# Moving the query and key transposes of a fused attention and MLP kernel from TensorE to the DMA engines

## The chip, the cores and the metric

The kernel runs on one core of one Trainium2 chip. The metric is the device time of one execution in microseconds (us). The executions of the kernel before lie within 0.5% of each other. Every ratio to the kernel before is of the same chip and the same rounds; where other runs are compared with each other or with the kernel after, they can be of different sessions, and the four sessions of the experiments were on four chips. The engines are named as the profile names them: PE is TensorE (PEld its weight loads), DVE is VectorE, ACT is ScalarE, POOL is GpSimd (its queue also issues DMAs that convert types) and SP is SyncE (its queue issues the other DMAs). L214 is line 214 of the kernel that the profile belongs to, so the same statement has other line numbers in other kernels.

## The reference

```python
def attention(q, k, v):                    # (8, 12, 448, 64), float32
    scores = (1 / sqrt(64)) * q @ k.T
    return (maximum(scores, 0) ** 2 / 448) @ v

x = attention(q, k, v)                     # heads side by side: (3584, 768)
out = maximum(x @ w_in, 0) ** 2 @ w_out    # w_in (768, 2048), w_out (2048, 768)
```

There is no softmax: attention is two matrix products with a squared ReLU between them, and the MLP has the same form.

## The kernel before

The work is ordered by batch (8) and pair of heads (6 a batch, so 48 pairs). For each pair, q and k come in as float32, are transposed on PE (so that the 64 head dimensions lie on partitions), and are copied by DVE into float16 tiles. Then come eight score matmuls (`sps`), a squared ReLU by ACT and DVE for each (`at`), and eight matmuls with v (`avps`). The MLP's matmuls (`hps` for the hidden layer, `ops` for the output) of earlier batches are a queue of filler that `fill` hands out between the attention's matmuls, so that PE has work while ACT and DVE are busy.

```python
    ps_p   = tile_pool(name="ps",   bufs=4, PSUM)   # sps, avps, hps: one bank each
    psmi_p = tile_pool(name="psmi", bufs=2, PSUM)   # tq, tk: one bank each
    pso_p  = tile_pool(name="pso",  bufs=1, PSUM)   # ops, 768 float32 columns: two banks
    FILL_RATIO = 1.5

    def attention_hp(b, hp):
        qst = qk_p.tile([SB, NSB, 2, D], FP32)      # SB = 112, NSB = 4
        kst = qk_p.tile([SB, NSB, 2, D], FP32)
        for j, vt in ((0, vA), (1, vB)):
            nc.sync.dma_start(out=qst[:, :, j, :], in_=q[b, 2*hp+j]...)
            nc.sync.dma_start(out=kst[:, :, j, :], in_=k[b, 2*hp+j]...)
            nc.gpsimd.dma_start(out=vt[...], in_=v[b, 2*hp+j, 0:384]...)
            nc.gpsimd.dma_start(out=vt[...], in_=v[b, 2*hp+j, 384:448])
        tq = psmi_p.tile([P, S], FP32)
        for i in range(NSB):
            nc.tensor.transpose(tq[:, i*SB:(i+1)*SB], qst[:, i], ident)
            fill(224)
        # two DVE copies into qTA and qTB (one head each, the other half zero), fill(500)
        # the same for kst: four transposes, one DVE copy into kT, fill(500)
        for c in range(4):
            for j, qT in ((0, qTA), (1, qTB)):
                sps = ps_p.tile([P, S], FP32)
                nc.tensor.matmul(sps, lhsT=kT[:, c*P:(c+1)*P], rhs=qT)
                # at <- sps by ACT and DVE
                fill(448)
        avps = ps_p.tile([P, S], FP32)
        # eight matmuls with v and at, fill(448) after each; ACT writes x
```

The PSUM has eight banks, and the three pools take all of them: 4 + 2 + 2. (The Trainium skill, "PSUM — Partial Sum Buffer", Specifications, gives 8 banks of 2 KiB a partition, so that the 768 float32 columns of `ops` need two.) A scheduler orders each engine's instructions when the kernel is built, by the readiness that it estimates, so the order in a queue is not the order of the source.

## Time and profile before

| | before |
|---|---|
| time, median of 6 runs at first (later sessions 538.07 to 539.49) | 538.97 us |
| PE busy | 500.0 of 538.4 us |
| start, batch 0's attention (cut at 63.7 us; its last `avps` ends at 65.0) | 63.7 us |
| middle, the 42 pairs of batches 1 to 7 (cut at 476.0 us; their last `avps` ends at 477.1) | 412.3 us |
| tail, MLP matmuls alone | 62.4 us |

The first lines are from the page of the kernel before: the span, PE's busy time with its share of the span and its count of instructions, and the engines' shares of the chain of work that ended last.

```profile
span 538.4 us, 8018 instructions
...
PE 500.0 (93%) x2816; PEld 281.6 (52%) x2816; DVE 373.4 (69%) x663; ACT 297.9 (55%) x589; POOL 138.4 (26%) x220
...
PE 87%; DMA 8%; ACT 2%; SPq 1%; DVE 1%; issue 0%; ACTq 0%
```

The windows view of the same kernel has the three stages. Its columns are the stretch in us, its length, each engine's busy time with its number of instructions, PE's granted clock (1.00 is full), the share of the DMA engines' time in use, and GB/s.

```profile
0.00:63.70 63.70, 38.20 (x148) 19.22 (x149) 37.95 (x72) 26.37 (x54) 30.66 (x56) 0.84 1.10 177
63.70:476.00 412.30, 409.43 (x2371) 233.37 (x2369) 324.89 (x576) 256.58 (x511) 107.77 (x164) 1.00 0.44 76
476.00:538.40 62.40, 52.38 (x300) 29.06 (x298) 10.60 (x18) 14.90 (x24) 0.00 (x0) 0.99 0.11 45
```

The profile counts PE as busy for 409 of the 412 us of the middle stage, so PE's work must shrink to save much time there. In the timeline of PE, each line is the start in us, the time taken, and what ran; x4 stands for four in a row.

```profile
206.62 0.35 PE L227 MATMUL sps<-qTA,kT 128*128 128x448 f16 x1
206.80 0.55 PE L217 MATMUL tk<-ident,kst 112*128 112x112 f32 x4
207.19 0.35 PE L227 MATMUL sps<-qTB,kT 128*128 128x448 f16 x1
```

The four transposes start at 206.80 and the next matmul at 207.19, so a transpose takes 0.097 us of PE, although the profile gives each one 0.27 us (its end is modelled and overlaps the next start). By the same reading a 448-column matmul takes 0.19 us, and 384 transposes take 37 us of the program's 473 us of PE work.

PE's waits after batch 0, from the table of waits with a window from 62 us to the end. The columns are the total in us, the number of waits and the longest.

```profile
PE ops L158 <- ACT osb L169: 7.4, 10, 0.9
PE sps L227 <- DVE at L114: 1.1, 6, 0.2
PE avps L236 <- DVE at L114: 0.2, 1, 0.2
```

Only one wait counts: `ops`, which has one PSUM buffer, waits for ACT to evict it. POOL waits for much longer (this line is for the whole program), but for nothing that holds anybody up: its v loads wait for the `avps` that used their tile.

```profile
POOL vf L197 <- PE avps L236: 273.2, 42, 9.4
```

### The profile page before, as it was taken

To read this page: it belongs to the slowest core of one execution; us is meant where nothing else is said; L and a number is where in the kernel's file an instruction comes from. 1 tells how busy PE (TensorE), PEld (TensorE's weight loads), DVE (VectorE), ACT (ScalarE), POOL (GpSimd) and SP (SyncE) were. 2 spreads that over 40 slices of the span, in tenths; PEclk is the share of its full clock that TensorE was granted. 3 is DMA by queue.
4 is the path that set the end of the run, shared out by engine and by line. 5 is a ranking of instruction groups with operands and counts; after the bars stand their busy time and mean duration, and the time that the engine had idled before them with its cause. 6 is when DMAs were issued, how large, how long until landed. Compare 5 with 4: busy or idle time off the path is not lost.

```text
span 538.4 us, 8018 instructions
## 1 busy us (share of the span) xinstructions
PE 500.0 (93%) x2816; PEld 281.6 (52%) x2816; DVE 373.4 (69%) x663; ACT 297.9 (55%) x589; POOL 138.4 (26%) x220
## 2 busy tenths in 40 slices
PE   1676999999999999999999999999999999999886
PEld 1333455555555555555555555555555555554553
DVE  2667788888887667898875667898875667764000
ACT  0444576667675546676745546675754555654111
POOL 7444311331133123213232123213232113000000
PEclk9968899999999999999999999999999999999999
DMA  9999534545355454343445454343545452100211
GB/s 162 199 205 197 79 50 72 82 86 93 62 85 89 95 119 67 46 78 47 82 89 104 93 118 66 48 69 51 78 96 94 106 109 36 10 0 3 86 60 59
DMA packets 142408, 45.36 MB, mean 84 GB/s; under 512 B 135968, under 2 KB 138016, under 8 KB 142368
## 3 DMA queue, kind: packets, MB, share of 16 engines
q1 hardware_dynamic: 93120, 33.04, 24.9%
q0 software_dynamic: 49248, 11.81, 22.6%
q8 instruction: 22, 0.36, 0.3%
q14 instruction: 18, 0.15, 0.1%
HBM read 45.61 MB, written 11.01 MB: 105 GB/s over the span
## 4 chain that ended last, share of the span: by engine, by line
PE 87%; DMA 8%; ACT 2%; SPq 1%; DVE 1%; issue 0%; ACTq 0%
PE hps L131 27%; PE ops L158 19%; PE sps L227 13%; PE avps L236 13%; PE ops L162 9%; DMA kst<-in_k_dram 6%; PE tq L208 3%; PE tk L217 3%; ACT osb L169 2%; DMA qst<-in_q_dram 2%; SPq L189 1%; ACT sq L113 1%; DVE at L114 1%; SPq L193 0%; ACTq L169 0%
## 5 line engine op out<-in xcount | busy, mean ns | idle before, releaser
L114 DVE SCALAR_TENSOR_TENSOR at<-sps,sq 128x448 f16<-128x448 f32 x384 | 216.1, 618 | 47.8 <-ACT sq L113 46.3
L113 ACT ACTIVATE sq<-sps 128x448 f16<-128x448 f32 x384 | 191.7, 550 | 78.3 <-PE sps L227 76.7
L131 PE MATMUL hps<-xt,w 128*128 128x448 f16 x768 | 188.0, 352 | 0.0
L158 PE MATMUL ops<-w,g 128*128 128x512 f16 x448 | 159.6, 379 | 7.6 <-ACT osb L169 7.4
L197 POOL DMA_DIRECT2D vf<-in_v_dram x96 | 74.2, 774 | 310.5 <-PE avps L236 273.2
L162 PE MATMUL ops<-w,g 128*128 128x256 f16 x448 | 122.0, 272 | 0.0
L236 PE MATMUL avps<-at,vf 128*128 128x448 f16 x384 | 111.3, 367 | 1.2 <-DVE at L114 1.0
L131 PEld LDWEIGHTS <-w 128*128 128x128 f16 x768 | 74.7, 97 | 69.7 <-issue 4.2
L113 ACT ACTIVATE sq<-hps 128x448 f16<-128x448 f32 x128 | 69.4, 542 | 58.2 <-PE hps L131 57.1
L114 DVE SCALAR_TENSOR_TENSOR g<-hps,sq 128x448 f16<-128x448 f32 x128 | 79.3, 620 | 32.0 <-ACT sq L113 31.7
L227 PE MATMUL sps<-qTA,kT 128*128 128x448 f16 x192 | 70.1, 365 | 1.6 <-DVE at L114 1.4
L227 PE MATMUL sps<-qTB,kT 128*128 128x448 f16 x192 | 69.9, 364 | 1.1 <-DVE at L114 1.1
L162 PEld LDWEIGHTS <-g 128*128 128x128 f16 x448 | 43.6, 97 | 34.5 <-issue 12.1
L158 PEld LDWEIGHTS <-g 128*128 128x128 f16 x448 | 43.5, 97 | 34.3 <-PE sps L227 0.4
L236 PEld LDWEIGHTS <-vf 128*128 128x128 f16 x384 | 38.6, 101 | 40.3 <-issue 8.6
L227 PEld LDWEIGHTS <-kT 128*128 128x128 f16 x384 | 36.8, 100 | 33.2 <-issue 6.2
L242 ACT ACTIVATE xt<-avps 128x448 f16<-128x448 f32 x48 | 26.0, 542 | 48.5 <-PE avps L236 48.0
L201 POOL DMA_DIRECT2D vf<-in_v_dram x96 | 52.3, 547 | 1.9 <-PE ops L158 0.9
L169 ACT ACTIVATE osb<-ops 128x768 f32<-128x768 f32 x28 | 22.8, 813 | 51.3 <-PE ops L162 51.3
L210 DVE TENSOR_SCALAR qTA<-tq 64x448 f16<-64x448 f32 x48 | 29.1, 606 | 29.7 <-PE tq L208 29.7
L208 PE MATMUL tq<-ident,qst 112*128 112x112 f32 x192 | 33.0, 269 | 14.0 <-DMA qst<-in_q_dram 13.2
L217 PE MATMUL tk<-ident,kst 112*128 112x112 f32 x192 | 35.5, 274 | 8.5 <-DMA kst<-in_k_dram 8.5
(17 smaller groups left out, 125.9 us busy)
## 6 DMA issues: line engine op xcount, KB each, us to landing
qst<-in_q_dram SPq DMA_DIRECT2D x96, 112.0 KB, 2.8
kst<-in_k_dram SPq DMA_DIRECT2D x96, 112.0 KB, 2.7
out_dram<-osb SPq DMA_DIRECT2D x28, 384.0 KB, 2.8
vf<-in_v_dram POOLq DMA_DIRECT2D x96, 48.0 KB, 2.6
w<-in_moe_w_in_dram POOLq DMA_DIRECT2D x6, 512.0 KB, 8.4
w<-in_moe_w_out_dram POOLq DMA_DIRECT2D x16, 192.0 KB, 8.3
vf<-in_v_dram POOLq DMA_DIRECT2D x96, 8.0 KB, 2.4
```

What stands on the lines that cost most here:

```text
L113: nc.scalar.activation(out=sq[:n], in_=src[:n], func=AF.Square)
L114: nc.vector.scalar_tensor_tensor(out=dst[:n], in0=src[:n], scalar=0.0, in1=sq[:n], op0=ALU.is_gt, op1=ALU.mult,)
L131: nc.tensor.matmul(hps[0], lhsT=w1[m][:, f * P : (f + 1) * P], rhs=xt[m][:, b * S : (b + 1) * S], start=(m == 0), stop=(m == NDMT - 1),)
L158: nc.tensor.matmul(ops[0][:, 0:512], lhsT=gt[f][:, rs], rhs=w2[f][:, 0:512], start=(f == 0), stop=(f == NFFT - 1),)
L162: nc.tensor.matmul(ops[0][:, 512:768], lhsT=gt[f][:, rs], rhs=w2[f][:, 512:768], start=(f == 0), stop=(f == NFFT - 1),)
L169: nc.scalar.activation(out=osb, in_=ops[0], func=AF.Copy, scale=CO)
L197: nc.gpsimd.dma_start(out=vt[:, 0:3, j * 64 : j * 64 + 64], in_=v[b, 2 * hp + j, 0:384].rearrange("(c p) d -> p c d", p=P),)
L201: nc.gpsimd.dma_start(out=vt[0:64, 3, j * 64 : j * 64 + 64], in_=v[b, 2 * hp + j, 384:448],)
L208: nc.tensor.transpose(tq[:, i * SB : (i + 1) * SB], qst[:, i], ident)
L217: nc.tensor.transpose(tk[:, i * SB : (i + 1) * SB], kst[:, i], ident)
L227: nc.tensor.matmul(sps, lhsT=kT[:, c * P : (c + 1) * P], rhs=qT, start=True, stop=True)
L236: nc.tensor.matmul(avps, lhsT=(vA if j == 0 else vB)[:, c, :], rhs=aa[2 * c + j], start=(c == 0 and j == 0), stop=(c == 3 and j == 1),)
```

## The change

The intent is to take the transposes away from PE. From batch 1 on, POOL's queue loads q and k with a conversion to float16, and a transposing DMA on SP's queue writes `qTA`, `qTB` and `kT` directly. Batch 0 keeps the transposes on PE. The tiles exist twice now, so that the next pair's can be prepared; the PSUM banks of the transposes go to a second `ops` buffer; and the fill ratio rises, because the fill calls between the transposes are gone.

```diff
-    psmi_p = tile_pool(name="psmi", bufs=2, PSUM)
-    pso_p = tile_pool(name="pso", bufs=1, PSUM)
+    pso_p = tile_pool(name="pso", bufs=2, PSUM)
-    FILL_RATIO = 1.5
+    FILL_RATIO = 2.15
+    # qkT[i] (128 x 1408) holds qTA, qTB, kT; qks[i] (112 x 12 x 128) the
+    # float16 q and k, with zeros where the other head is; i = 0, 1
+    def prefetch(u):                       # u = pair, 0 to 47
+        b, hp = divmod(u, NHP)
+        i = u % 2
+        for j, st in ((0, qsA[i]), (1, qsB[i])):
+            # b == 0: as before, float32 on SP
+            nc.gpsimd.dma_start(out=st[:, :, j*64:j*64+64], in_=q[b, 2*hp+j]...)
+            nc.gpsimd.dma_start(out=ks[i][:, :, j*64:j*64+64], in_=k[b, 2*hp+j]...)
+            nc.gpsimd.dma_start(...)       # v, two loads as before
+        if b == 0: return
+        nc.sync.dma_start_transpose(qkT[i][:, 0:3*S]..., qks[i]...)
-    def attention_hp(b, hp):
+    def attention_hp(u):
+        if u + 1 < B * NHP:
+            prefetch(u + 1)
+        if b == 0:
+            # transposes on PE and three DVE copies, without fill calls
         ... scores, squared ReLU, avps as before, on qTA[i], qTB[i], kT[i], vA[i], vB[i]
```

(Cuts are marked by dots and comments. The scale of 256 moves from the copy of k into ACT's square; that changes no instruction's size.)

More of the change, by code (lines that the diff above doesn't have):

```diff
@@ L42 @@
     NFFT = FF // P
-    NRB = S // SB
-    SK = 256.0
+    SSQ = 256.0
     CX = 1.0 / 896.0
@@ L49 @@
     const_p = ctx.enter_context(tc.tile_pool(name="const", bufs=1))
+    qk_p = ctx.enter_context(tc.tile_pool(name="qkp", bufs=2))
     w_p = ctx.enter_context(tc.tile_pool(name="wp", bufs=1))
     xt_p = ctx.enter_context(tc.tile_pool(name="xtp", bufs=1))
-    qk_p = ctx.enter_context(tc.tile_pool(name="qkp", bufs=2))
     qkt_p = ctx.enter_context(tc.tile_pool(name="qktp", bufs=1))
@@ L59 @@
     ps_p = ctx.enter_context(tc.tile_pool(name="ps", bufs=4, space=bass.MemoryType.PSUM))
-    psmi_p = ctx.enter_context(tc.tile_pool(name="psmi", bufs=2, space=bass.MemoryType.PSUM))
-    pso_p = ctx.enter_context(tc.tile_pool(name="pso", bufs=1, space=bass.MemoryType.PSUM))
+    pso_p = ctx.enter_context(tc.tile_pool(name="pso", bufs=2, space=bass.MemoryType.PSUM))
     ident = const_p.tile([SB, SB], FP32, name="ident", tag="ident")
     make_identity(nc, ident)
+    staged = {}
     w1 = [w_p.tile([P, FF], FP16, name=f"w1_{i}", tag=f"w1_{i}")
@@ L79 @@
         xt.append(xt_p.tile([P, NT], FP16, name=f"xt_{i}", tag=f"xt_{i}"))
-    qTA = qkt_p.tile([P, S], FP16, name="qTA", tag="qTA")
-    qTB = qkt_p.tile([P, S], FP16, name="qTB", tag="qTB")
-    kT = qkt_p.tile([P, 512], FP16, name="kT", tag="kT")
-    nc.vector.memset(qTA[64:128, :], 0.0)
-    nc.vector.memset(qTB[0:64, :], 0.0)
-    nc.vector.memset(kT[:, 448:512], 0.0)
-    vfx = []
-    for i in range(4):
-        t = qkt_p.tile([P, NCH, P], FP16, name=f"vf_{i}", tag=f"vf_{i}")
-        nc.vector.memset(t, 0.0)
-        vfx.append(t)
+    qkT, qks = [], []
+    qTA, qTB, kT, qsA, qsB, ks, vA, vB = ([], [], [], [], [], [], [], [])
+    for i in range(2):
+        qkT.append(qkt_p.tile([P, 3 * S + 64], FP16, name=f"qkT{i}", tag=f"qkT{i}"))
+        qks.append(qkt_p.tile([SB, 3 * NSB, P], FP16, name=f"qks{i}", tag=f"qks{i}"))
+        qTA.append(qkT[i][:, 0:S])
+        qTB.append(qkT[i][:, S : 2 * S])
+        kT.append(qkT[i][:, 2 * S : 2 * S + 512])
+        qsA.append(qks[i][:, 0:NSB])
+        qsB.append(qks[i][:, NSB : 2 * NSB])
+        ks.append(qks[i][:, 2 * NSB : 3 * NSB])
+        vA.append(qkt_p.tile([P, NCH, P], FP16, name=f"vA{i}", tag=f"vA{i}"))
+        vB.append(qkt_p.tile([P, NCH, P], FP16, name=f"vB{i}", tag=f"vB{i}"))
+        nc.vector.memset(qTA[i][64:128, :], 0.0)
+        nc.vector.memset(qTB[i][0:64, :], 0.0)
+        nc.vector.memset(kT[i][:, 448:512], 0.0)
+        nc.vector.memset(qsA[i][:, :, 64:128], 0.0)
+        nc.vector.memset(qsB[i][:, :, 0:64], 0.0)
+        nc.vector.memset(vA[i], 0.0)
+        nc.vector.memset(vB[i], 0.0)
     fifo: deque = deque()
     deficit = 0.0
-    FILL_RATIO = 1.5
+    FILL_RATIO = 2.15
     def fill(cycles):
@@ L109, in drain_fifo, with relu2_psum_to_sbuf @@
             fifo.popleft()()
-    def relu2_psum_to_sbuf(dst, src, n):
+    def relu2_psum_to_sbuf(dst, src, scale):
         sq = sq_p.tile([P, S], FP16, name="sq", tag="sq")
-        nc.scalar.activation(out=sq[:n], in_=src[:n], func=AF.Square)
+        nc.scalar.activation(out=sq, in_=src, func=AF.Square, scale=scale)
         nc.vector.scalar_tensor_tensor(
-            out=dst[:n], in0=src[:n], scalar=0.0, in1=sq[:n],
+            out=dst, in0=src, scalar=0.0, in1=sq,
             op0=ALU.is_gt, op1=ALU.mult,
@@ L140, in run @@
                     relu2_psum_to_sbuf(gt[f][:, (b % 2) * S : (b % 2 + 1) * S],
-                                       hps[0], P)
+                                       hps[0], 1.0)
                 return 448
@@ L181, in moe_o_block @@
                 yield o_mm(tb, f)
-    def attention_hp(b, hp):
-        qst = qk_p.tile([SB, NSB, 2, D], FP32, name="qst", tag="qst")
-        kst = qk_p.tile([SB, NSB, 2, D], FP32, name="kst", tag="kst")
-        vA = vfx[2 * (hp % 2)]
-        vB = vfx[2 * (hp % 2) + 1]
-        for j, vt in ((0, vA), (1, vB)):
-            nc.sync.dma_start(
-                out=qst[:, :, j, :],
+    def prefetch(u):
+        b, hp = divmod(u, NHP)
+        i = u % 2
+        if b == 0:
+            staged[u] = [qk_p.tile([SB, NSB, 2, D], FP32, name=n, tag=n)
+                         for n in ("qst", "kst")]
+        for j, st in ((0, qsA[i]), (1, qsB[i])):
+            if b == 0:
+                for t, src in zip(staged[u], (q, k)):
+                    nc.sync.dma_start(
+                        out=t[:, :, j, :],
+                        in_=src[b, 2 * hp + j].rearrange("(sb p) d -> p sb d", p=SB))
+            else:
+              nc.gpsimd.dma_start(
+                out=st[:, :, j * 64 : j * 64 + 64],
                 in_=q[b, 2 * hp + j].rearrange("(sb p) d -> p sb d", p=SB),
             )
-            nc.sync.dma_start(
-                out=kst[:, :, j, :],
+              nc.gpsimd.dma_start(
+                out=ks[i][:, :, j * 64 : j * 64 + 64],
                 in_=k[b, 2 * hp + j].rearrange("(sb p) d -> p sb d", p=SB),
@@ L197, in attention_hp @@
             nc.gpsimd.dma_start(
-                out=vt[:, 0:3, j * 64 : j * 64 + 64],
+                out=(vA[i] if j == 0 else vB[i])[:, 0:3, j * 64 : j * 64 + 64],
                 in_=v[b, 2 * hp + j, 0:384].rearrange("(c p) d -> p c d", p=P),
@@ L201, in attention_hp @@
             nc.gpsimd.dma_start(
-                out=vt[0:64, 3, j * 64 : j * 64 + 64],
+                out=(vA[i] if j == 0 else vB[i])[0:64, 3, j * 64 : j * 64 + 64],
                 in_=v[b, 2 * hp + j, 384:448],
             )
-        tq = psmi_p.tile([P, S], FP32, name="tq", tag="psmi")
-        for i in range(NSB):
-            nc.tensor.transpose(tq[:, i * SB : (i + 1) * SB], qst[:, i], ident)
-            fill(224)
-        nc.vector.tensor_scalar(out=qTA[0:64, :], in0=tq[0:64, :],
-                                scalar1=1.0, scalar2=None, op0=ALU.mult)
@@ L212, in attention_hp @@
-        nc.vector.tensor_scalar(out=qTB[64:128, :], in0=tq[64:128, :],
-                                scalar1=1.0, scalar2=None, op0=ALU.mult)
-        fill(500)
-        tk = psmi_p.tile([P, S], FP32, name="tk", tag="psmi")
-        for i in range(NSB):
-            nc.tensor.transpose(tk[:, i * SB : (i + 1) * SB], kst[:, i], ident)
-            fill(224)
-        nc.vector.tensor_scalar(out=kT[:, 0:448], in0=tk, scalar1=SK,
-                                scalar2=None, op0=ALU.mult)
-        fill(500)
+        if b == 0:
+            return
@@ new lines, in prefetch @@
+        nc.sync.dma_start_transpose(
+            qkT[i][:, 0 : 3 * S].rearrange("p (s r) -> p s r", s=3 * NSB),
+            qks[i].rearrange("r s c -> r (s c)"))
+    def attention_hp(u):
+        b, hp = divmod(u, NHP)
+        i = u % 2
+        if u + 1 < B * NHP:
+            prefetch(u + 1)
+        if b == 0:
+            qst, kst = staged.pop(u)
+            tq = ps_p.tile([P, S], FP32, name="tq", tag="ps")
+            for s in range(NSB):
+                nc.tensor.transpose(tq[:, s * SB : (s + 1) * SB], qst[:, s], ident)
+            nc.vector.tensor_copy(out=qTA[i][0:64, :], in_=tq[0:64, :])
+            nc.vector.tensor_copy(out=qTB[i][64:128, :], in_=tq[64:128, :])
+            tk = ps_p.tile([P, S], FP32, name="tk", tag="ps")
+            for s in range(NSB):
+                nc.tensor.transpose(tk[:, s * SB : (s + 1) * SB], kst[:, s], ident)
+            nc.vector.tensor_copy(out=kT[i][:, 0:S], in_=tk)
@@ L223, in attention_hp @@
         aa = []
         for c in range(NCH):
-            for j, qT in ((0, qTA), (1, qTB)):
+            for j, qT in ((0, qTA[i]), (1, qTB[i])):
                 sps = ps_p.tile([P, S], FP32, name=f"sps{j}", tag="ps")
-                nc.tensor.matmul(sps, lhsT=kT[:, c * P : (c + 1) * P], rhs=qT,
-                                 start=True, stop=True)
+                nc.tensor.matmul(sps, lhsT=kT[i][:, c * P : (c + 1) * P],
+                                 rhs=qT, start=True, stop=True)
                 at = attn_p.tile([P, S], FP16, name=f"at{j}", tag="at")
-                relu2_psum_to_sbuf(at, sps, P)
+                relu2_psum_to_sbuf(at, sps, SSQ)
@@ L236, in attention_hp @@
                 nc.tensor.matmul(
-                    avps, lhsT=(vA if j == 0 else vB)[:, c, :],
+                    avps, lhsT=(vA[i] if j == 0 else vB[i])[:, c, :],
                     rhs=aa[2 * c + j],
@@ L245, in attention_hp @@
         )
+    prefetch(0)
     for b in range(B):
         for hp in range(NHP):
-            attention_hp(b, hp)
+            attention_hp(b * NHP + hp)
             if b == 0:
```

## The prediction

> **What bounds it now.** The page shows PE busy 500.0 of 538.4 us (93%) and 87% of the chain that ended last. By spacing of starts in the timeline, a 448-column matmul takes 0.19 us, a 512 plus 256 pair 0.33 us, a float32 transpose 0.097 us (four in 0.55 us). Over the program: 436 us of matmuls and 384 x 0.097 = 37 us of transposes, 473 us. The rest is the start (up to 62 us, DMA-limited: DMA share above 1.0 in the windows table, waits of 17 and 15 us for kst in the chain), about 16 us of small stalls up to 477 us, and ten 0.7 us waits of ops for ACT's osb (7.4 us).
>
> **What the change does.** In batches 1 to 7 (42 of 48 head pairs) the 8 transposes per pair go, 336 x 0.097 = 33 us of PE, and three DVE copies (0.61 + 0.63 + 0.62 us per pair, 78 us of DVE off the critical path). The second ops buffer removes most of the 7.4 us. The fill ratio only makes up for lost fill calls (2.15 x 7168 against 1.5 x 9960 cycles a pair). Batch 0 and the weight loads stay, so the start stays near 60 to 65 us. If nothing else bound: 490 to 500 us.
>
> **What it adds.** q and k move from SP to POOL as casting loads, and each pair needs one DMA transpose (344 KB). In the built order POOL's queue puts pair u+1's v loads before most of its q/k loads, and the v loads wait for pair u-1's last avps (POOL waits 273 us for that now, harmlessly). So a chain appears: avps(u-1) ends; four v issues (0.77 and 0.54 us each, 2.6 us) and three q/k issues (0.82 us, estimated from the v issues' slope); the last k load lands 2.6 us after its issue (v's median): 7.2 us. Then the transpose, T. Only then may sps of u+1 start. PE's own work per pair, by its built order, is 9 to 11 us with filler and 5 to 6 us at the ends of odd batches. Pairs u-1 and u+1 alternate buffers, so the period is the larger of the PE work and (7.2 + T + work)/2. Stepped over 42 pairs: 517 us at T = 2, 529 at 3, 546 at 4, 567 at 5; some 15 us less if 7.2 is 6.
>
> T is unknown: this trace has no transpose DMA. The Trainium skill, "DMA: Bandwidth & Descriptors", "Latency and other measured facts", gives 261 GB/s for one with a non-contiguous middle dimension: 1.3 us, an estimate. Its section "Anatomy of one DMA" gives about 2 us of fixed cost; this trace agrees (8 KB v loads land in 2.4 us). So T is about 3.3 us, with a tail upward.
>
> **Prediction.** The PE gain is real, but part is handed back as waits of sps for the transpose: 520 us, 8 in 10 between 495 and 572. Faster by over 2%: 0.58; within 2%: 0.14; slower: 0.28.
>
> **What would show it.** PE busy down about 35 us; tq and tk with 24 matmuls each; DVE busy down 75 to 80; ops no longer waits for ACT. In the waits, a large new one: sps or its weight load waiting for the DMA into qkT, worst in pairs with little filler. POOL busy near 275 us. The chain shows the transpose and the q/k loads.
>
> **What would make it wrong.** T of 5 us or more (small packets, engines shared with loads) makes it slower; T near 2 us gives 500 to 515. A start delayed by q/k behind weights in POOL's queue, or transposes held behind output stores on SP, would add.

## The result, and the profile after

The kernel after takes 494.23 us (median of 8 runs, 492.17 to 495.96), against 539.17 us for the kernel before (16 runs). The ratio is 0.917, with a 95% interval of 0.915 to 0.918. The results are correct. The direction was forecast; the time lies just below the stated range of 495 to 572 us, and the gain is 45 us in place of the forecast 19 us.

From the page of the kernel after, the lines that answer to those above:

```profile
span 492.3 us, 7247 instructions
...
PE 465.0 (94%) x2480; PEld 244.3 (50%) x2480; DVE 303.9 (62%) x544; ACT 299.2 (61%) x589; POOL 255.6 (52%) x388
...
PE 89%; DVE 4%; ACT 3%; DMA 3%; issue 1%; SPq 0%; ACTq 0%
```

The windows view of the kernel after, with its own three stages:

```profile
0.00:62.40 62.40, 40.24 (x146) 16.91 (x147) 39.99 (x80) 27.76 (x55) 39.40 (x69) 0.87 1.25 178
62.40:438.00 375.60, 374.76 (x2044) 199.11 (x2043) 253.87 (x448) 256.57 (x511) 216.23 (x320) 1.00 0.86 96
438.00:492.30 54.30, 50.02 (x293) 28.30 (x290) 10.01 (x16) 14.91 (x24) 0.00 (x0) 1.00 0.13 51
```

The start is nearly as long as before (62.4 against 63.7 us). The middle stage is 36.7 us shorter, and the tail 8.1 us. (Cut in both kernels at the ends of the last `avps` of batch 0 and of batch 7, the three stages are 2.4, 36.7 and 7.0 us shorter.) The DMA share of the middle stage doubles, from 0.44 to 0.86, and yet PE is busy for 374.8 of 375.6 us. PE's table of waits from 62 us to the end, which showed 8.7 us before, has no line at all in the kernel after; this is its heading with nothing below it:

```profile
core 0 of [0], span 492.3 us
engine line waited for: us in total, times, longest us
```

So the wait that the prediction was built on, `sps` for the transposing DMA, does not exist. The transposes themselves are not fast. The first line below is from the view of their line in the kernel after (duration of the issue on SP in ns, minimum, median and maximum), and the second is their time from issue to landing in us:

```profile
L222 SPq DMA_TRANSPOSE qkT<-qks x42: 1260/1391/2645, 50.1 to 415.5; - x42
...
DMA to landing us min/median/max: 3.4/4.4/7.5
```

They take 4.4 us in the median, longer than the 3.3 us assumed. They are only started early enough. Three stretches of the timeline of the kernel after show it. The first is PE around one pair; call the pair whose scores end at 203.63 A, the next one B, and the one after that C. (Each attention line is one matmul.)

```profile
198.28 0.35 PE L246 MATMUL sps<-qkT 128*128 128x448 f16 x1
...
203.63 0.35 PE L246 MATMUL sps<-qkT 128*128 128x448 f16 x1
...
208.76 0.35 PE L255 MATMUL avps<-at,vB 128*128 128x448 f16 x1
...
209.33 0.35 PE L246 MATMUL sps<-qkT 128*128 128x448 f16 x1
...
215.59 0.35 PE L246 MATMUL sps<-qkT 128*128 128x448 f16 x1
```

The scores of A run from 198.28 to 203.98 us, its `avps` ends at 209.1, the scores of B begin at 209.33 and those of C at 215.59. SP in the same stretch:

```profile
204.02 1.35 SPq L222 DMA_TRANSPOSE qkT<-qks  x1
```

This transpose is issued 0.04 us after the last score of A. It writes the tile that A has just finished reading, so it is C's. It lands 3.5 us later, and C's scores begin 11.6 us after its issue. Over all 42 transposes, paired with their scores in this way, the lead of the issue over the first score is 14.2 us in the median and 6.7 us at least. Most are issued within 0.1 us of the last score of the pair two before, the rest within 1 us, and every one before that pair's `avps` has ended. POOL in the same stretch shows why the loads are never late:

```profile
196.66 0.76 POOL L212 DMA_DIRECT2D vA<-in_v_dram  x1 [3.95 <-PE avps L255]
198.10 0.74 POOL L204 DMA_DIRECT2D qks<-in_q_dram  x1 [0.68 <-DMA qkT<-qks]
...
202.06 0.73 POOL L208 DMA_DIRECT2D qks<-in_k_dram  x1
...
208.02 0.71 POOL L204 DMA_DIRECT2D qks<-in_q_dram  x1 [5.24 <-DMA qkT<-qks]
```

At 198.10, while A's scores have only begun, POOL issues q and k of D (three pairs on), and at 208.02 q of the pair after D, 0.5 us after C's transpose has landed and freed its staging tile. The v loads between them, which began at 196.66 when the `avps` before A's gave their tile back, are those of B. So the loads of q and k run two pairs ahead of the v loads that stand beside them in the queue. POOL's largest waits in the kernel after say the same: POOL waits for transposes to free the staging tile, and for `avps` 30 us in place of 273.

```profile
POOL qks L204 <- DMA qkT<-qks: 113.0, 32, 6.3
...
POOL vA L212 <- PE avps L255: 30.0, 10, 7.2
```

The other effects came near the forecast. PE busy fell by 35.0 us (forecast 35), DVE busy by 69.5 (75 to 80), POOL busy rose to 255.6 (275; the casting q and k issues take 0.72 us each, 0.82 was assumed), and `tq` and `tk` have 24 matmuls each.

### The profile page after: what moved, and what is told of

The parts are those of the page before. It is cut to its first block, busy times and chain, and to the rows that moved or that the text cites. A ratio compares the mean times of both kernels' runs of the same rounds, so it can differ in the third digit from the quotient of the medians.

```text
span 492.3 us, 7247 instructions
## 1 busy us (share of the span) xinstructions
PE 465.0 (94%) x2480; PEld 244.3 (50%) x2480; DVE 303.9 (62%) x544; ACT 299.2 (61%) x589; POOL 255.6 (52%) x388
## 4 chain that ended last, share of the span: by engine, by line
PE 89%; DVE 4%; ACT 3%; DMA 3%; issue 1%; SPq 0%; ACTq 0%
PE hps L139 29%; PE ops L166 19%; PE avps L255 15%; PE sps L246 15%; PE ops L170 10%; DVE at L122 2%; ACT sq L121 2%; DMA vA<-in_v_dram 1%; DMA qst<-in_q_dram 1%; PE tq L235 1%; DVE qkT L241 1%; DVE qkT L237 1%; DVE qkT L236 1%; ACT xt L261 1%; ACT osb L177 0%
## 5 line engine op out<-in xcount | busy, mean ns | idle before, releaser
L246 PE MATMUL sps<-qkT 128*128 128x448 f16 x384 | 134.5, 365 | 12.2 <-DVE qkT L241 7.4
L204 POOL DMA_DIRECT2D qks<-in_q_dram x84 | 60.4, 719 | 114.6 <-DMA qkT<-qks 113.0
L255 PE MATMUL avps<-at,vA 128*128 128x448 f16 x192 | 70.6, 368 | 1.4 <-DMA vA<-in_v_dram 0.7
L255 PE MATMUL avps<-at,vB 128*128 128x448 f16 x192 | 70.4, 367 | 0.0
L246 PEld LDWEIGHTS <-qkT 128*128 128x128 f16 x384 | 37.5, 99 | 52.3 <-issue 13.2
L208 POOL DMA_DIRECT2D qks<-in_k_dram x84 | 60.5, 720 | 0.8 <-issue 0.7
L212 POOL DMA_DIRECT2D vA<-in_v_dram x48 | 36.2, 753 | 33.1 <-PE avps L255 30.0
L177 ACT ACTIVATE osb<-ops 128x768 f32<-128x768 f32 x28 | 22.9, 819 | 44.1 <-PE ops L170 44.1
L212 POOL DMA_DIRECT2D vB<-in_v_dram x48 | 36.5, 761 | 1.7 <-issue 0.7
L255 PEld LDWEIGHTS <-vA 128*128 128x128 f16 x192 | 19.3, 100 | 23.4 <-issue 4.0
L255 PEld LDWEIGHTS <-vB 128*128 128x128 f16 x192 | 19.2, 100 | 20.5 <-issue 3.5
```

The lines of the kernel that those rows point to most:

```text
L177: nc.scalar.activation(out=osb, in_=ops[0], func=AF.Copy, scale=CO)
L204: nc.gpsimd.dma_start(out=st[:, :, j * 64 : j * 64 + 64], in_=q[b, 2 * hp + j].rearrange("(sb p) d -> p sb d", p=SB),)
L208: nc.gpsimd.dma_start(out=ks[i][:, :, j * 64 : j * 64 + 64], in_=k[b, 2 * hp + j].rearrange("(sb p) d -> p sb d", p=SB),)
L212: nc.gpsimd.dma_start(out=(vA[i] if j == 0 else vB[i])[:, 0:3, j * 64 : j * 64 + 64], in_=v[b, 2 * hp + j, 0:384].rearrange("(c p) d -> p ...
L246: nc.tensor.matmul(sps, lhsT=kT[i][:, c * P : (c + 1) * P], rhs=qT, start=True, stop=True)
L255: nc.tensor.matmul(avps, lhsT=(vA[i] if j == 0 else vB[i])[:, c, :], rhs=aa[2 * c + j], start=(c == 0 and j == 0), stop=(c == 3 and j == 1),)
```

## The experiments

All sixteen ran on the chip with three rounds beside the kernel before, whose median was 538.07 to 539.49 us in those sessions. Granted clocks are the means of the profiled execution. Two theories stood against each other at first. A: the prediction's chain is right as arithmetic, but was built on a wrong reading of the queue's order; in truth each transpose has a lead of some 14 us, so its 4.4 us cost nothing. B: the order and the lead don't matter. How the 45 us divide was the second question.

| run | median, us | ratio to before |
|---|---|---|
| (kernel after) | 494.23 | 0.917 |
| gate_qk | 571.94 | 1.061 |
| one_qkT | 525.29 | 0.974 |
| transpose_twice | 503.64 | 0.934 |
| double_transpose | 605.96 | 1.124 |
| pe_transposes | 556.20 | 1.032 |
| psum_only | 548.94 | 1.018 |
| one_ops | 510.57 | 0.948 |
| six_ps | 501.64 | 0.929 |
| fill_150 | 503.01 | 0.933 |
| dma_all | 517.09 | 0.960 |
| w2_late | 494.93 | 0.919 |
| w2_late_v4 | 493.98 | 0.916 |
| w2_late_v4_dma_all | 502.07 | 0.933 |
| v4_pipe | 494.56 | 0.917 |
| w2_late_v4_pipe | 494.83 | 0.917 |
| w2_late_v4_pipe_act | 488.45 | 0.907 |

### Building the chain of the prediction (gate_qk)

```diff
+        if b > 0:
+            pb, php = divmod(u - 2, NHP)
+            nc.gpsimd.tensor_scalar(out=qks[i][0:1, :, 0:128:64],
+                in0=xt[php][0:1, pb*S : pb*S+24]..., scalar1=0.0, op0=ALU.mult)
         for j, st in ((0, qsA[i]), (1, qsB[i])):
```

The tiny write lands in cells that the q and k loads then overwrite, or that are zero anyway, so the result is unchanged, but the loads must wait for the eviction of the `avps` two pairs before.

> The kernel after, with one tiny GpSimd write ahead of each pair's q and k loads that reads x of the pair two before (so it waits until that pair's avps has ended and ScalarE has evicted it). This builds the chain of the prediction: q/k loads of u+1 only after avps of u-1. Theory A (the prediction's chain was right arithmetic on a wrong queue order: in the kernel after, q/k loads run two pairs ahead of the v loads, the transpose is issued 0.04 us after the last sps two pairs before and has a lead of 14 us over its use): sps now waits for the transpose in most pairs, time 525 to 565 us, transposes issued about 6 us after the end of avps two pairs before instead of 4 us ahead of it. Theory B (queue order is immaterial, transposes would be hidden either way): within 1% of 494 us.

The time is 571.94 us, so B is refuted, and A's range was a little too low. Three stretches of its timeline show one pair. PE's timeline of gate_qk has the last `avps` of two pairs before (from 335.52) and the first scores that use the transpose:

```profile
335.52 0.35 PE L262 MATMUL avps<-at,vB 128*128 128x448 f16 x1
...
348.09 0.36 PE L253 MATMUL sps<-qkT 128*128 128x448 f16 x1 [2.36 <-DMA qkT<-qks]
```

POOL's timeline of gate_qk has the gate and the first load behind it:

```profile
336.93 0.35 POOL L199 TENSOR_SCALAR qks<-xt 1x24 f16<-1x24 f16 x1
337.57 0.76 POOL L211 DMA_DIRECT2D qks<-in_q_dram  x1 [0.30 <-POOL qks L199]
```

SP's timeline of gate_qk has the transpose:

```profile
343.77 1.36 SPq L229 DMA_TRANSPOSE qkT<-qks  x1
```

The transpose is issued 7.9 us after that `avps` ended (335.87); over all 42 pairs the median is 7.5 us, against 7.2 us in the prediction's sum. It lands 4.3 us later, and PE has then sat idle for 2.36 us. In total PE waited for the transposes as follows in gate_qk:

```profile
PEld L253 <- DMA qkT<-qks: 58.0, 22, 5.8
...
PE sps L253 <- DMA qkT<-qks: 48.6, 19, 5.4
```

(The two lines are largely the same waits, once at the weight load and once at the matmul.) So the waits of the prediction's chain were priced about right; the chain is just not in the kernel after. The total was not: the transposes took 3.5 us in the median here, for which the prediction's table gives between 529 and 546 us. Most of what lies above that goes with a lower granted clock, which the prediction did not have: its mean was 0.927, against 0.983 in the kernel after, and PE busy was 490.4 us in place of 465.0 for the same matmuls. That the idle gaps lowered the clock was not tested by itself.

### Shrinking the lead, and doubling the landing time (one_qkT, transpose_twice, double_transpose)

```diff
 # one_qkT: both parities use one transposed tile
-        qkT.append(qkt_p.tile([P, 3 * S + 64], FP16, name=f"qkT{i}", tag=f"qkT{i}"))
+        qkT.append(qkt_p.tile(..., name="qkT0", tag="qkT0") if i == 0 else qkT[0])
 # transpose_twice: the same transpose again, into the same tile
+        for _ in range(2):
             nc.sync.dma_start_transpose(qkT[i]..., qks[i]...)
 # double_transpose: another one ahead of it, into a tile that nobody reads
+        nc.sync.dma_start_transpose(scr..., qks[i]...)
         nc.sync.dma_start_transpose(qkT[i]..., qks[i]...)
```

> The kernel after with one transposed tile for both parities, so that the transpose of u can start only after the last sps of u-1; its lead over sps of u shrinks from about 14 us to the length of the avps phase, 4.5 us with filler and 2.2 us without. Theory A: full pairs wait about 0 to 0.5 us, the dozen short ones 2 to 3 us: 505 to 530 us. Theory B (nothing depends on the lead): 494 us.

It took 525.29 us, inside A's range. Its result is wrong: the source writes the next pair's tile before this pair's scores read it, so with one tile each pair computes with the next pair's q and k. For timing it serves, because each transpose still waits for the last score that reads the tile, and the next score waits for the transpose. The share of the transposing DMA in the chain of work that ended last is 18% there.

> The scratch run before this one put the extra transpose of the next pair ahead of the real one in SP's queue, so it tested queue order and not landing time. Here the same transpose is issued twice into the same tile, the second after the first has landed, so one pair's transposed q and k arrive about 8.8 us after issue in place of 4.4. Theory A (lead 14 us in the median over the first sps, 7 to 9.5 us in about a fifth of the pairs): only pairs at the ends of odd batches wait, 494 to 515 us. If the lead were really used up: half of 4.4 us for each of 42 pairs, about 585 us.

It took 503.64 us, inside the range: the traffic of the transposes doubled, landing took twice as long (9.1 us in the median from the first issue to the second landing), and 9 us of 45 were lost. PE's waits in transpose_twice hold only four for the transposes:

```profile
PE sps L247 <- DMA qkT<-qks: 6.3, 4, 3.1
```

> The kernel after, with a second DMA transpose of the same pair into a scratch tile issued ahead of the real one. Theory A (lead of 14 us in the median, 6.7 us at least, against 4.4 us to landing): time within 1.5% of 494 us, although the transposes' traffic doubles. If landing times or engine share had been what limits: each of 42 pairs later by up to 2 to 4 us, 530 us or more.

This one, run before transpose_twice, missed by far: 605.96 us. It was a bad experiment, and a telling one. The built order of SP's queue in double_transpose (the numbers of pairs are added here) has, after the scratch transpose of pair 6:

```
DmaTransposeAnt scr <- qks1     pair 7, scratch: waits for the loads of pair 7
DmaTransposeAnt qkT0 <- qks0    pair 6, the real one
DmaTransposeAnt scr <- qks0     pair 8, scratch: waits for the loads of pair 8
DmaTransposeAnt qkT1 <- qks1    pair 7, the real one
```

The scratch transpose doesn't wait for any score, so the scheduler put it ahead of the real transpose of the pair before. The real one then waits behind the loads of the following pair, and the loads of the pair after that wait for the real one to free the staging tile. That is a chain of the same kind as in gate_qk, made by the order of one queue, so this run says nothing about traffic. transpose_twice has the same traffic and lost 9 us, so the traffic accounts for that much at most.

### Dividing the gain (pe_transposes, psum_only, one_ops, six_ps, fill_150)

```diff
 # pe_transposes: the kernel after, batch 0's way of transposing in every batch
-        if b == 0:
+        if True:                                  (four places)
 # psum_only: the kernel before with the PSUM part of the change
-    psmi_p = tile_pool(name="psmi", bufs=2, PSUM)
-    pso_p = tile_pool(name="pso", bufs=1, PSUM)
+    pso_p = tile_pool(name="pso", bufs=2, PSUM)
-        tq = psmi_p.tile(...)                     (tk too)
+        tq = ps_p.tile(..., tag="ps")
 # one_ops: the kernel after with one ops buffer
-    pso_p = tile_pool(name="pso", bufs=2, PSUM)
+    pso_p = tile_pool(name="pso", bufs=1, PSUM)
 # six_ps: one_ops, and ps bufs=6 in place of 4
 # fill_150: the kernel after with FILL_RATIO = 1.5
```

> The kernel after with the PE transposes and the staged float32 loads of batch 0 in all batches (no DMA transposes, q and k on SP), all else (two ops buffers, fill ratio 2.15, PSUM from one pool) kept. If the transposes off PE are the main gain: 33 us of PE come back, 525 to 532 us, and the remaining 7 to 14 us of the 45 gained are the PSUM change and the rest. Rival (the PSUM buffers and the ratio are the main gain): 505 us or less.

It took 556.20 us, outside both ranges. It isn't a clean undo: batch 0's way has no fill calls between transposes, so PE stands still for the DVE copies in all batches (16.2 us of waits of `sps` for `qkT` copies, in 20 places, and 33.6 us at the weight loads). The transposes are worth more than their 33 us if nothing covers the copies behind them.

> The kernel before with only the PSUM part of the change: transposes share the pool of four with sps and hps, and ops gets two buffers. If the second ops buffer is what the change's PSUM part is worth: 7 us faster than before, 530 to 533 us. Rival (PE transposes sharing the pool make sps and hps wait, so that this layout only pays once the transposes are off PE): as slow as before or slower, 540 to 555 us.

It took 548.94 us: the rival was right, and the PSUM part by itself is a loss of 1.8%. With it the waits for ACT are gone, but `tq` and `tk` now take buffers from `sps` and `hps`, and PE waits for DVE instead. From 62 us to the end, PE's waits in psum_only are:

```profile
PE sps L226 <- DVE kT L218: 4.1, 9, 1.4
PE sps L226 <- DVE at L113: 3.4, 12, 0.7
```

The sum of these waits is only some 8 us, about what the evictions cost before; the middle stage, cut at the ends of `avps` as above, is nonetheless 431.4 us long, against 412.1, with 403.0 us of PE work by spacing, against 399.0. The rest of that loss is in small gaps between matmuls that no wait in the table names, and I did not follow them further.

> The kernel after with one ops buffer in place of two (everything else kept). If the second buffer is worth its waits (7.4 us in the kernel before, 0 in the kernel after): 500 to 503 us, with ops waiting for the eviction again. Rival (PE has other work to do then): 494 us.

It took 510.57 us, so the second `ops` buffer is worth 16.3 us in the kernel after, more than twice the 7.4 us seen in the waits. The waits in one_ops are those of the kernel before again, and some more of `sps` behind them:

```profile
PE ops L166 <- ACT osb L177: 6.7, 10, 0.9
PE sps L246 <- DVE at L122: 3.0, 10, 0.5
```

The tail of one_ops takes 60.8 us and its middle 385.6, against 54.3 and 375.6 in the kernel after: 6.5 and 10.0 us. In the middle, the loss sits in a few pairs: four of the 42 take 1.3 to 2.3 us more than their PE work by spacing, the others 1.0 at most; in the kernel after none takes more than 0.6. That a wait in the table is smaller than the loss is seen in the tail of the kernel before. Two lines of PE's timeline there:

```profile
527.38 0.27 PE L162 MATMUL ops<-w,g 128*128 128x256 f16 x1
528.60 0.38 PE L158 MATMUL ops<-w,g 128*128 128x512 f16 x1 [0.95 <-ACT osb L169]
```

Matmuls there start 0.11 or 0.22 us apart. Across the eviction the starts are 1.22 us apart, so the step costs 1.1 us; the table counts 0.95, from the modelled end of the last matmul.

> The kernel after with one ops buffer, and the two PSUM banks so freed given to the pool of sps, hps and avps (6 in place of 4). If PSUM space as such was worth 16 us: about 494 us. If only a second ops buffer removes those waits: 508 to 512 us, as with one ops buffer and four.

It took 501.64 us, between the two: the two banks are worth 9 us as score buffers and 16 us as a second `ops` buffer. The traces show where the two uses differ. Over the middle stage six_ps takes 7.4 us more than its PE work by spacing, about as the kernel after (8.0), where one_ops takes 17.9: there two more banks do as well in either pool. Its tail keeps the six waits of `ops` (5.6 us, as in one_ops) and takes 11.0 us more than its work, against 4.5 in the kernel after; and batch 0 ended 2.7 us later than in the kernel after, for which I have no cause.

> The kernel after with the fill ratio of the kernel before (1.5 in place of 2.15). By the built order the pairs then hold 7.6 to 9.2 us of PE work where they are filled (9.5 to 10.9 before), and the undisturbed tail grows from 50 to 97 us of PE work; the total is the same. If the ratio only makes up for the lost fill calls and PE is busy either way: within 1.5% of 494 us. Rival (pairs with less filler run into ScalarE, VectorE or GpSimd, or into shorter leads): 505 us or more.

It took 503.01 us, just over the range for "no matter". So the ratio is more than a make-up for lost calls, but it's worth 9 us at most: the pairs of fill_150 lose 16 us in all against their PE work by spacing (8 in the kernel after), mostly spread thinly.

Together: with the transposes on DMA, the new fill ratio and one `ops` buffer as before, 539 becomes 510.6 us (28.5 us). With the second `ops` buffer, 510.6 becomes 494.2 (16.3 us). With the transposes on PE, the same PSUM layout makes 539 into 549. So the second buffer pays where the transposes need no PSUM, and did not in the one layout tried in which they do.

### The start (dma_all, w2_late, w2_late_v4, w2_late_v4_dma_all, v4_pipe, w2_late_v4_pipe, w2_late_v4_pipe_act)

The prediction called the first 62 us DMA-limited. The change left them as they were, and they are what remains: the 96 matmuls and 48 transposes of batch 0 are some 23 us of PE work by the spacing above (96 x 0.19 + 48 x 0.097), in over 60 us.

```diff
 # dma_all: DMA transposes in batch 0 too
-        if b == 0:
+        if False:                                 (four places)
 # w2_late: half of the weight bytes meant to come later (see below)
             if b == 0:
                 load_weights(hp)                  # now w1 alone
+            if b == 1:
+                load_w2(hp)
 # v4: four v tiles
-        vA.append(...)                            # i = 0, 1, used as vA[i]
+        vA.append(...)                            # 0 to 3, used as vA[u % 4]
 # pipe: in batch 0, the next pair's scores ahead of this pair's avps
-            attention_hp(b * NHP + hp)
+            aa = attention_front(u)
+            if hp: attention_back(u - 1, held)
+            held = aa
 # act: in batch 0, one of three copies to ACT
-            nc.vector.tensor_copy(out=qTB[i][64:128, :], in_=tq[64:128, :])
+            nc.scalar.activation(out=qTB[i][64:128, :], in_=tq[64:128, :], func=AF.Copy)
```

> The kernel after with the DMA transposes in batch 0 too (no PE transposes at all). Tests why the change left batch 0 alone. If the start is limited by VectorE work in series (the chain of waits shows three qkT copies of 0.63 us in each pair): up to 10 us faster, 484 to 490 us. If the casting loads of q and k queue behind the weights there: start longer by 5 to 20 us, 500 to 515 us.

It took 517.09 us: the loads of q and k queue behind the weights in batch 0, PE waits 44.1 us for six transposes, and batch 0 ends at 79.3 us. This is what the change avoids by its special case.

> The kernel after with the w2 loads (half of the weight bytes, first used only in batch 2) issued in batch 1 in place of batch 0. The first 62 us are not changed by the change (62 us both times) and DMA share is above 1 there. If weights' bytes limit the start: start 8 to 14 us shorter, 480 to 487 us. Rival (the start is limited by VectorE's work and landing latencies, or the w2 loads then hold q, k and v back in batch 1): 490 us or more.

It took 494.93 us: nothing gained. But the edit did not take the bytes out of batch 0. The scheduler moved the w2 loads forward again, as the view of their line in w2_late shows (times of the issues at the end):

```profile
L75 POOL DMA_DIRECT2D w<-in_moe_w_out_dram x16: 528/534/562, 31.9 to 48.5; - x16
```

All 16 landed before batch 0 ended, at 61.5 us (in the kernel after they were issued from 8.8 to 48.3 us), and the DMAs moved 11.1 MB in the first 62 us in both kernels. So this run says nothing about the weights' bytes. The chain of waits held an 8 us wait for v in batch 0.

> The run with w2 loaded late still waited 8 us for v of the last pair of batch 0, which is issued only when the pair two before is done and then lands behind weights. Here four v tiles in place of two let it be issued earlier, with w2 late as well. If that wait is all: 485 to 488 us. Rival (another wait takes its place): 492 us or more.

It took 493.98 us: that wait is gone, and batch 0 ended at 63.2 us all the same.

> Late w2, four v tiles and DMA transposes in batch 0 together. If weights no longer hold the casting loads back, each pair of batch 0 loses about 1.9 us of VectorE copies in series: 476 to 484 us. If q and k loads still queue behind w1: 490 us or more.

It took 502.07 us: better than dma_all. Here the w2 loads did come late (issued from 60.7 to 92.5 us), and batch 0 ended at 62.5 us in place of 79.3; but PE still waits 22.3 us for five transposes in batch 0, whose loads stand between those of w1 in POOL's queue, and 5.3 us for w2 after it.

> The kernel after with four v tiles, and in batch 0 the scores of the next pair ahead of avps of this one. If batch 0 is a series of VectorE (7 us a pair) and avps (2.7 us a pair, waiting for the last at): avps then hides, start 52 to 56 us, 484 to 488 us. If the weights' bytes set the start: 62 us, 492 to 496 us.

> The same with w2 loaded in batch 1. If the series was all: as v4_pipe, within 1%. If bytes come next once the series is gone: start shorter than v4_pipe's by 3 us or more.

They took 494.56 and 494.83 us: nothing again, and batch 0 ended at 62.4 us in both. So the order of scores and `avps` does not set the start by itself. The second run did not test the bytes, since its w2 loads were issued from 34.2 to 52.6 us.

> The same with one of the three copies per pair of batch 0 on ScalarE (VectorE 6.2 us a pair, ScalarE 6.1). If VectorE sets the pace of batch 0: 3 to 4 us less than w2_late_v4_pipe.

It took 488.45 us. With one copy of 0.63 us a pair off DVE (3.8 us over batch 0), batch 0 ended at 54.8 us in the profiled execution, 7.6 us earlier. The windows of the start show what else changed. The third number from the right is PE's granted clock. First the windows of w2_late_v4_pipe:

```profile
0.00:20.00 20.00, 7.94 (x28) 3.66 (x29) 12.09 (x33) 6.03 (x12) 15.65 (x30) 0.95 1.19 168
20.00:40.00 20.00, 14.36 (x52) 5.94 (x51) 13.94 (x26) 10.34 (x23) 12.23 (x20) 0.76 1.36 193
40.00:62.00 22.00, 16.74 (x65) 7.44 (x65) 14.95 (x27) 10.93 (x22) 13.30 (x23) 0.80 1.29 178
```

And the windows of w2_late_v4_pipe_act:

```profile
0.00:20.00 20.00, 9.77 (x30) 4.50 (x31) 11.94 (x33) 8.36 (x16) 15.39 (x29) 1.00 1.16 164
20.00:40.00 20.00, 15.05 (x67) 7.13 (x65) 14.38 (x28) 12.33 (x25) 12.57 (x20) 1.00 1.39 192
40.00:55.00 15.00, 10.46 (x50) 4.87 (x51) 10.43 (x20) 9.99 (x21) 8.65 (x17) 1.00 1.35 185
```

The clock reads 0.76 and 0.80 in one and 1.00 in the other. That 1.00 holds only from 24.9 us on, where the record of the clock begins in this trace (14.5 us in the other): the view counts the clock as full before its first record, but the matmuls were slow until then, as PE's timeline of w2_late_v4_pipe_act shows.

```profile
23.88 0.58 PE L265 MATMUL avps<-at,vB 128*128 128x448 f16 x1
```

From 24.9 us on the clock stays full in w2_late_v4_pipe_act, and falls to half three times in w2_late_v4_pipe. The matmuls of `avps` (shape 128 x 448) in batch 0 follow it: the view of their line gives a median of 0.55 us each in w2_late_v4_pipe, and 0.35 us in w2_late_v4_pipe_act (columns: count, then minimum, median and maximum in ns, and when they ran). First w2_late_v4_pipe:

```profile
L265 PE MATMUL avps<-at,vB x23: 350/551/578, 22.8 to 61.6; 128*128 128x448 f16 x23
```

The same view of w2_late_v4_pipe_act:

```profile
L265 PE MATMUL avps<-at,vB x24: 350/352/577, 21.6 to 54.5; 128*128 128x448 f16 x24
```

So PE runs slowly through part of the start of the kernel before (0.84), the kernel after (0.87) and the other runs, and its short bursts wait for DVE, as the last run suggests. The Trainium skill, "TensorE: Matmul & The Clock Gate", Part 1, says that TensorE's clock drops to half after an idle window of about 3.4 us and rises after a busy one. The trace of the kernel after agrees on the two speeds and on the step: from 18.6 us, where its record begins, the windows view gives 0.50 for 22.0 to 25.4, 39.1 to 42.5, 45.9 to 49.3 and 56.2 to 63.0 us, and 0.99 or 1.00 between. But "idle" is not "without work" here: in the 3.4 us before each of the four drops PE was busy for 1.2 to 1.6 us, and after the first load no gap of PE is longer than 1.5 us. How much of the 7.6 us is the shorter series on DVE, and how much the clock, these runs don't separate: the copies explain 3.8 us. The profiled execution is also the fastest of four (486.85 us at a mean clock of 1.000; the others 488.37 to 490.20 us at 0.987 to 0.991). One of these, at 0.987, has a span of 488.4 us, and one of w2_late_v4_pipe at 0.985 has 492.7 us: at nearly the same mean clock some 4 us remain, about what the copies explain.

w2_late_v4_pipe_act beats both kernels: 0.907 of the time before (95% interval 0.905 to 0.909), against 0.917 for the kernel after.

## Why the prediction was right or wrong

- **"PE busy down about 35 us; tq and tk with 24 matmuls each; ops no longer waits for ACT."** Right: 35.0 us, 24 each, and no such wait.
- **"If nothing else bound: 490 to 500 us."** Right: 494.23 us, and from 62 us on PE waits for nothing that the table names.
- **"In the built order POOL's queue puts pair u+1's v loads before most of its q/k loads."** This is the step that failed. Beside the v loads of pair u+1 stand the q and k loads of pair u+3. I read the built order by tile names; tiles alternate between two buffers, so the names of pairs u+1 and u+3 are the same, and in batch 0 v goes through POOL's queue while q and k don't, which fits the shift of the two streams by two pairs (I did not test that as its cause). The wait that I put ahead of the transpose was thus two pairs away, and the transpose is issued about 4.3 us before `avps` two pairs back ends (median), and not 7.2 us after. It should have been checked by counting the issues from the start of the queue.
- **"avps(u-1) ends ... 7.2 us. Then the transpose, T."** Right as a price of the chain: gate_qk, which builds it, issues its transposes 7.5 us after (median). That its 572 us also lie near the prediction's dearer cases is luck in part: at the 3.5 us that T was there, the prediction's table gives 529 to 546 us, and about 25 us are PE work at a lower clock.
- **"T is about 3.3 us, with a tail upward."** Too low: 4.4 us in the median in the kernel after (3.4 to 7.5). "T of 5 us or more makes it slower" was wrong: transpose_twice, with about twice the T, is at 503.64 us, still 7% faster than before.
- **"The second ops buffer removes most of the 7.4 us."** Mis-sized: removing it from the kernel after costs 16.3 us (6.5 in the tail, 10.0 in the middle). The table's idle time leaves out part of the step between starts, and a stall at the head of PE's queue also holds up the matmuls behind it, whose `sps` then wait for DVE, as one_ops suggests; in the middle, two more score buffers remove the loss as well (six_ps).
- **"33 us of PE"** for the transposes: right as PE work (the spacing sums of the middle stage fall from 399.2 to 367.7 us). With one `ops` buffer as before, and the new fill ratio, the move is worth 28.5 us.
- **"The fill ratio only makes up for lost fill calls."** Nearly: 1.5 in place of 2.15 costs 8.8 us.
- **"The start stays near 60 to 65 us."** Right: 62.4 us. **"DMA-limited"** fits the kernel before, where DMAs make up 66% of the first 62 us of the chain of work that ended last, and PE waited 21.7 us for q and k loads. It fits the kernel after poorly: DMAs are 21% of that stretch of its chain, and PE waits 9.8 us for them there, of which 8.0 are for the first load of q, and 12.2 us for DVE. Taking waits for v out didn't shorten the start, and taking DVE work out did, at a higher clock. What fewer bytes would give stays open: no run took them out of a batch 0 that kept its PE transposes, and the DMA share there is above 1.

## What to carry to other kernels

Whether a slow transfer costs anything is a matter of its lead: find what its issue waits for, and how long before its use that is, by counting instructions in the built queue and not by tile names, which repeat with every turn of the buffers. An in-order queue makes any instruction's wait the wait of all behind it, so one extra transfer or one gate can cost over 70 us where a doubled transfer time costs 9. When work leaves an engine, look at what memory it gives back: the PSUM banks of the departed transposes were worth a third of the gain as a second output buffer, and were a loss while the transposes still needed them.

## What the Trainium skill lacked or had wrong

- "DMA: Bandwidth & Descriptors", Latency and other measured facts: 261 GB/s for a transposing DMA, with the fixed 2 us of its section Anatomy of one DMA, led to 3.3 us for 344 KB; measured from issue to landing were 3.4 to 7.5 us, median 4.4, beside other DMAs (and 3.5 us in the median in gate_qk, where the DMA engines were less used: a share of 0.72 in the middle stage against 0.86). The 2 us are given there for DMAs that GpSimd issues, and these transposes are issued on SP, so the sum was my estimate and not the page's. The page has no duration from issue to landing for such a transpose between tiles in SBUF, nor a time that one of this size occupies SP's queue (1.4 us here).
- "DMA: Bandwidth & Descriptors", Anatomy of one DMA: descriptor generation on GpSimd is called small and variable, without a time. Here each casting load of q, k and v occupied POOL for 0.56 us (64 contiguous pieces), 0.72 us (448 pieces) or 0.76 us (384 pieces), and 382 loads, nearly all of POOL's 388 instructions, made POOL busy for 255.6 of 492.3 us.
- "TensorE: Matmul & The Clock Gate", Part 4: it gives 275 to 390 ns for one transpose (bfloat16, 128 x 128), but no cost in a stream. Four float32 transposes of 112 x 112 among other matmuls start 0.097 us apart.
- The same page, Part 1, has a clock of two states and a window of about 3.4 us, but not how much work a window may hold and still count as idle. In the kernel after the clock fell after windows with 1.2 to 1.6 us of busy PE, and stayed full after one with 1.95 us (25.4 to 28.8 us). The 448-column `avps` matmuls of batch 0 have medians of 0.48 to 0.58 us in all kernels here but one, in place of 0.35.
